# Attention and two expert layers on one core: a list scheduler orders the first phase, a fourth unit moves to TensorE, value products of two heads take half the array each

## The chip, the cores and the metric

The kernel runs on one core of a Trainium2 chip. The time is that of the device for one execution, in microseconds (us). Before the change the median of three runs is 878.46 us (876.66 to 881.11). TensorE is called PE, VectorE DVE, ScalarE ACT, GpSimd POOL, and SyncE SP.

## What is computed

Four batches, eight heads, 576 positions, head width 64. Attention has two parts that are added. The pooled part averages four neighbouring positions of q, k and v, attends over all 144 of them, and repeats each result four times. The local part attends within three positions to either side. The rows then pass two feed-forward layers, one with the maximum of three products and one with a leaky maximum:

```python
out_d = sm_attn(q_d, k_d, v_d)              # q_d, k_d, v_d: means over 4 positions
out_up = np.repeat(out_d, 4, axis=2)
mask = np.abs(pos[:, None] - pos[None, :]) < 4
out_local = softmax(where(mask, q @ k.T / 8, -1e9)) @ v
x = (out_up + out_local) as 2304 rows of 512
h = np.maximum(np.maximum(x @ w1, x @ w2), x @ w3)    # 512 -> 768
x = h @ w_out                                         # 768 -> 512
h = x @ w_in                                          # 512 -> 2048
out = np.maximum(0.01 * h, h) @ w_out2                # 2048 -> 512
```

Weights and activations are split into a high and a low part of a shorter float type, and a product is three matmuls: high by high, high by low, low by high.

## The kernel before, in words

Phase 1 is attention and the first feed-forward layer pair; phase 2 is the second one. The 2304 rows are eight units of 288, two for each batch. A unit has 18 groups of 12 matmuls into `ps_h` (`L1_mm`, line 709: six blocks `m` of the hidden width, three weights `e` each), the maxima over the three on DVE (`L1_post`, the tile `hm`), and then four groups of 18 matmuls into `ps_o` (`L2`, line 740), whose results go to memory as `x2d`. Phase 2 reads `x2d` in chunks of 512 rows (`L3`, `L4`), and `L4` (line 811) stores the result.

The input of a unit comes from two kinds of local attention:

- Units 0, 1 and 2 (`PEU = 3`) do it on PE, for four head pairs `h`. The calls of one pair are one chain: `pl_C` (line 384: a band matmul for each of two heads into `ps_ls`, then the products of q and k), `pl_D` (DVE, maxima), `pl_E` (ACT, exponentials), `pl_H` (DVE), `pl_I` (POOL, division), `pl_O` (PE transposes into `ps_lt`), `pl_o` (DVE), `pl_P` (line 467: products with the values `sv` into `ps_lo`, two PSUM banks of the pool `mm`, one for each head, each with 128 rows of which 64 are used), `pl_Q` (line 479, DVE, adds the pooled part, two instructions), `pl_R` (ACT), `pl_S` (POOL). The first-layer groups of a unit read what `pl_R` and `pl_S` write.
- Units 3 to 7 do it with long element operations, 32 rows by four heads at once: `qk_mult` (POOL), `qk_reduce` (DVE and ACT), `sm1` and `sm2` (softmax), `pv_mult` and `pv_sum` (DVE, the tiles `pvprod` and `O`). `emit_T` (line 656) then turns `O` on PE into `ps_x`, and DVE adds the pooled part and splits the result into `xh` and `xl`. The weights `lp` of the first of these units lie in SBUF, those of the others in PSUM (line 275).

The pooled part of a batch and head pair is one chain too: `ds_pool_qk`, `ds_B` (line 540, PE, into `ps_sc`), `ds_F`, `ds_G`, `ds_J`, `ds_norm`, `ds_M` (transposes), `ds_m`, `ds_N` (line 615, products with the pooled values into `ps_up`, 128 rows of which 64 are used for each head), `ds_v`.

The order has two sources. The start of the program (unit 0's chains, eight weight conversions) is written out by hand in `ORDER`, for every engine. For the rest the calls are emitted by a table of places (`at`, `TURN`, `DONE`, `DS0`, `B1`), one place for each group of first- or second-layer matmuls, and only SP keeps that order; on PE, DVE, ACT and POOL the framework's scheduler orders the instructions by its own timeline. The four banks of `mm` serve `ps_h`, `ps_o` and `ps_lo` in turn.

Of the kernel before, what the change touches and what calls it, by code (L numbers as in the profile page):

```python
# [41 lines left out]
PEU = 3  # L42
ML = 2
SUPA = 16
SUPB = 36
# [13 lines left out]
FILL1 = 8  # L59

DONE = {3: 56, 4: 81, 5: 102, 6: 122, 7: 143}
TURN = {3: 60, 4: 83, 5: 104, 6: 125, 7: 146}

B1 = (12, 16, 20, 24)
B1OFF = dict(A=0, v=1, C=1, B=2, L=4, O=4, M=7, P=7, N=9, Q=10)
DS0 = {2: (39, 46, 53, 60), 3: (68, 79, 90, 101)}
DSOFF = (0, 5, 6, 9, 10, 11, 16, 20)
ON_A = (0, 21, 14)
# [3 lines left out]
def local_global_attention_moe_kernel(  # L72
# [66 lines left out]
    pools = {0: sup, 1: supb}  # L139

    bands = []
    for u in range(2):
        bd = pools[1 - u].tile([QB, NBLK, KB], BF16, name=f"band{u}")
        P.memset(bd, 0.0)
        edge = 0 if u == 0 else NBLK - 1
        conds = [(0, NBLK, 1, -1, 0), (0, NBLK, -1, 1, KB - QB)]
        conds.append((edge, 1, 1, 0, -(FAC - 1)) if u == 0 else (edge, 1, -1, 0, KB - FAC))
        for j0, n, step, cm, base in conds:
            P.affine_select(
                out=bd[:, j0 : j0 + n], in_=bd[:, j0 : j0 + n], pattern=[[0, n], [step, KB]], base=base,  # L150
                channel_multiplier=cm, compare_op=ALU.is_ge, fill=-(2.0**33),
            )
        bands.append(bd)
# [202 lines left out]
    def pl_load(what, b, h):  # L356
        if what == "a":
            t = pools[b].tile([128, 2 * S + 6], F32, tag="sqk", bufs=2 if b else 4, name="sqk")
            nc.sync.dma_start(out=t, in_=qk[b, h])
            dst[b, h, "q"], dst[b, h, "k"] = halves(t)  # L360
            pl[b, h, "q"], pl[b, h, "k"] = t[:, :S], t[:, S:]
        elif what == "s":
            n = PEU - 2 * b if b else 2
            t = pools[b].tile([KP, n, NBLK, 128], F32, tag="sv", bufs=2 if b else 4, name="sv")
            nc.sync.dma_start(
                out=t.rearrange("p u n d -> p (u n d)"), in_=vW[b, h][:, : n * NBLK * 128]
            )
            pl[b, h, "v"] = t
# [15 lines left out]
    def pl_C(u, h):  # L384
        qr, kr = pl[u // 2, h, "q"], pl[u // 2, h, "k"]
# [30 lines left out]
    def pl_E(u, h):  # L416
        n = NBLK * KB
        pst, nm = pl[u, h, "ps"], pl.pop((u, h, "nm"))
        if u == 0:
            et = late_tile([QB, 2, NBLK, KB], "ple")  # L420
        else:
            et = pools[u // 2].tile([QB, 2, NBLK, KB], F32, tag="ple", bufs=3 - u, name="ple")
        pl[u, h, "e"] = et
        sm = pl[u, h, "sum"] = pools[u // 2].tile([QB, 2, NBLK], F32, tag="plsm", bufs=4, name="plsm")
# [41 lines left out]

    def pl_P(u, h):
        t = pl.pop((u, h, "aT"))
        ps = pl[u, h, "o"] = [scratch(u, "mm", "ps_lo") for hh in range(2)]
        if u == 0:  # L470
            fill("P", ps[0])
# [184 lines left out]
    def emit_T(u):  # L656
# [395 lines left out]
```

## Time and profile before

| | us |
|---|---|
| median of three runs | 878.46 |
| the profiled execution | 879.78 |
| its span, first to last instruction | 878.0 |
| phase 1, to the last second-layer matmul | 0 to 469.8 |
| phase 2, to the last matmul | 469.8 to 867.9 |
| after the last matmul | 867.9 to 878.0 |
| PE busy | 833.8 (95%) |
| DVE, ACT, POOL busy | 471.9, 413.4, 260.1 |

The rows further down are lines of the profile. A row of the time order gives the start, the length, the engine, the source line, what is written and read, shapes (partitions x elements) and how many instructions stand together; in square brackets stands the idle time before it and what ended that. Matmuls overlap, so a call's cost is best read from one start to the next. A matmul on four-byte floats of the plain kind shows as two instructions.

### The profile page before, as it was taken

Reading aid. Unit: us, or ns where it says so; the run is one execution under the profiler, and the core shown is the slowest. Engines: PE = TensorE matmul, PEld = TensorE weight load, DVE = VectorE, ACT = ScalarE, POOL = GpSimd, SP = SyncE. Lnnn points to the kernel's source line nnn. Section 1 sums busy time; section 2 is a strip of 40 time slices with the busy share of each in tenths; the row PEclk is TensorE's granted clock in tenths of the full one; section 3 lists DMA queues with packets and bytes.
Section 4 is the critical chain, followed back from the end, with each engine's and each line's share of the span. In section 5 each row is a group of like instructions: output and inputs, shape, how many; then the busy total and the mean of one; then the engine's idle time right before and its main releaser. Section 6 shows DMA issues by size and latency. Waiting matters only on the chain.

```text
span 878.0 us, 13769 instructions
## 1 busy us (share of the span) xinstructions
PE 833.8 (95%) x5009; PEld 734.0 (84%) x5009; DVE 471.9 (54%) x912; ACT 413.4 (47%) x1556; POOL 260.1 (30%) x240
## 2 busy tenths in 40 slices
PE   8989997799999798999999999999999999999995
PEld 4778886799999698999998888888888888788894
DVE  6778758767767887422764995332233222322221
ACT  5788686536476585221654884322223222322221
POOL 6757796379658891101020000000000000000000
PEclk8989998699999899999999999999999999999998
DMA  9681422305233330130316800200021001100100
GB/s 279 247 341 26 164 80 70 112 24 171 99 108 110 120 97 28 29 128 6 107 77 242 360 1 1 84 13 1 1 64 33 1 1 36 36 1 1 29 20 24
DMA packets 27342, 73.98 MB, mean 84 GB/s; under 512 B 3082, under 2 KB 8138, under 8 KB 27274
## 3 DMA queue, kind: packets, MB, share of 16 engines
q1 hardware_dynamic: 22666, 68.38, 22.6%
q10 hardware_dynamic: 4608, 4.72, 1.5%
q8 instruction: 39, 0.64, 0.3%
q14 instruction: 29, 0.24, 0.1%
HBM read 63.65 MB, written 9.44 MB: 83 GB/s over the span
## 4 chain that ended last, share of the span: by engine, by line
PE 75%; DMA 8%; DVE 5%; ACT 4%; POOL 4%; issue 2%; SPq 1%; ACTq 0%; DVEq 0%; POOLq 0%
PE acc L820 22%; PE ps_g L796 22%; PE ps_h L717 19%; PE ps_o L747 6%; POOL qkprod L254 3%; DMA lk<-in_kL_dram 2%; ACT qkprod L267 2%; DMA dsrawv<-in_vP_dram 2%; PE ps_lo L474 1%; DMA raw<-x2d 1%; DMA wO<-in_w_out_dram 1%; PE ps_up L622 1%; DMA sv<-in_vW_dram 1%; PE ps_sc L548 1%; PE ps_ls L399 1%
## 5 line engine op out<-in xcount | busy, mean ns | idle before, releaser
L717 PE MATMUL ps_h<-xh,wA 128*128 128x288 f32 x1152 | 204.5, 307 | 10.6 <-DVE x L489 4.7
L717 PEld LDWEIGHTS ps_h<-xh,wA 128*128 128x128 f32 x1152 | 173.5, 195 | 15.8 <-DVE x L489 5.0
L820 PE MATMUL acc<-w2o,gh 128*128 128x512 f32 x576 | 178.0, 391 | 0.8 <-ACT gh L807 0.8
L796 PE MATMUL ps_g<-x2h,w2i 128*128 128x512 f32 (+1 forms) x640 | 158.9, 370 | 0.0
L804 DVE TENSOR_TENSOR g<-g,ps_g 128x512 f32<-128x512 f32 (+1 forms) x80 | 50.7, 634 | 189.0 <-ACT g L803 188.9
L803 ACT ACTIVATE g<-ps_g 128x512 f32<-128x512 f32 (+1 forms) x80 | 44.3, 553 | 190.2 <-PE ps_g L796 190.1
L796 PEld LDWEIGHTS ps_g<-x2h,w2i 128*128 128x128 f32 x640 | 114.6, 188 | 22.9
L820 PEld LDWEIGHTS acc<-w2o,gh 128*128 128x128 f32 x576 | 106.9, 188 | 23.2 <-ACT gh L807 1.2
L717 PE MATMUL ps_h<-xl,wA 128*128 128x288 f32 x576 | 113.2, 303 | 0.5 <-POOL xl L499 0.5
L820 PE MATMUL acc<-w2o,gl 128*128 128x512 f32 x288 | 112.1, 391 | 0.0
L254 POOL TENSOR_TENSOR qkprod<-lq,lk 128x1344 f32<-128x1344 f32 x30 | 91.8, 3072 | 8.6 <-DVE O L308 4.9
L717 PEld LDWEIGHTS ps_h<-xl,wA 128*128 128x128 f32 x576 | 91.3, 195 | 1.0 <-POOL xl L499 0.7
L267 ACT ACTIVATE qkprod<-qkprod 128x64 f32<-128x64 f32 x350 | 84.4, 248 | 14.4 <-POOL qkprod L254 14.3
L796 PE MATMUL ps_g<-x2l,w2i 128*128 128x512 f32 (+1 forms) x320 | 79.6, 370 | 0.0
L734 DVE TENSOR_TENSOR hm<-hm,ps_h 128x288 f32<-128x288 f32 x96 | 43.0, 448 | 67.3 <-PE ps_h L717 64.3
L747 PE MATMUL ps_o<-hh,wO 128*128 128x288 f32 x384 | 76.8, 297 | 0.0
L738 POOL TENSOR_TENSOR hl<-hm,hh 128x288 fp32r<-128x288 f32 x48 | 40.5, 846 | 116.9 <-ACT hh L737 116.9
L808 DVE TENSOR_TENSOR gl<-g,gh 128x512 fp32r<-128x512 f32 (+1 forms) x80 | 51.0, 637 | 39.6 <-ACT gh L807 35.1
L267 ACT ACTIVATION_READ_ACCUMULATOR qkprod<-qkprod 128x1 f32 x350 | 67.8, 194 | 0.0
L807 ACT ACTIVATE gh<-g 128x512 fp32r<-128x512 f32 (+1 forms) x80 | 47.0, 588 | 42.5 <-DVE g L804 42.1
L796 PEld LDWEIGHTS ps_g<-x2l,w2i 128*128 128x128 f32 x320 | 56.8, 188 | 10.9
L820 PEld LDWEIGHTS acc<-w2o,gl 128*128 128x128 f32 x288 | 54.1, 188 | 12.2 <-DVE gl L808 0.4
(131 smaller groups left out, 1157.8 us busy)
## 6 DMA issues: line engine op xcount, KB each, us to landing
wA<-in_wa_dram SPq DMA_DIRECT2D x18, 512.0 KB, 10.7
w2i<-in_w_in_dram SPq DMA_DIRECT2D x16, 512.0 KB, 7.5
w2o<-in_w_out_dram SPq DMA_DIRECT2D x16, 512.0 KB, 8.7
dsrawv<-in_vP_dram SPq DMA_DIRECT2D x16, 320.0 KB, 8.5
lk<-in_kL_dram SPq DMA_DIRECT2D x10, 480.0 KB, 6.9
lv<-in_vL_dram SPq DMA_DIRECT2D x10, 480.0 KB, 4.0
sqk<-in_qk_dram SPq DMA_DIRECT2D x8, 579.0 KB
dsraw<-in_qk_dram SPq DMA_DIRECT2D x8, 579.0 KB, 4.5
```

The costliest lines, as they stand in the source:

```text
L254: P.tensor_tensor(out=pr, in0=in0, in1=in1, op=ALU.mult)
L267: A.activation(out=pr[:, r, j], in_=pr[:, r, j], func=AF.Copy, accum_out=sc[:, r, j : j + 1])
L717: T.matmul(out=ps, lhsT=wA[m, e][wi][:, kk * 128 : kk * 128 + 128], rhs=xx[:, kk] if u < PEU else xx[:, :, kk, :], start=n == 0, stop=n == ...
L734: V.tensor_tensor(out=t, in0=t, in1=ps, op=ALU.max)
L738: P.tensor_tensor(out=hl[:, m], in0=t, in1=hh[:, m].bitcast(F32), op=ALU.subtract)
L747: T.matmul(out=ps, lhsT=wO[m][wi][:, os_], rhs=xx[:, m], start=n == 0, stop=n == 3 * M1 - 1)
L796: T.matmul(out=ps, lhsT=w2i[m][wi][:, kk * 128 : kk * 128 + 128], rhs=xx[:, kk, :n], start=j == 0, stop=j == 3 * KC - 1,)
L803: A.activation(out=g, in_=ps, func=AF.Copy, scale=0.01)
L804: V.tensor_tensor(out=g, in0=g, in1=ps, op=ALU.max)
L807: A.activation(out=gh, in_=g, func=AF.Copy)
L808: V.tensor_tensor(out=gl, in0=g, in1=gh.bitcast(F32), op=ALU.subtract)
L820: T.matmul(out=accs[c, t], lhsT=a[:, ts], rhs=w, start=m == 0 and j == 0, stop=m == M2 - 1 and j == 2)
```

## The change

- `PEU` becomes 4: unit 3's local attention is done on PE, in pair calls as units 1 and 2. The units with long element operations are 4 to 7, and the first of these, with weights in SBUF, is unit 4.
- After the start that `ORDER` writes out, a class `Plan` orders phase 1 for all five engines. Each call is a step with an engine, a length, the steps it needs, and buffers that it holds from its first step to a last one. Due times come from the table `LEN` (one pace for each unit) and are carried back along the chains; `SHIFT` moves them by kind and `SLACK` says how long before its due time a kind may begin. The engine that is free takes the ready step that is due first. The chip gets the order, not the times.
- `pl_P` and `ds_N` write two heads into the two halves of one bank, with 64 columns of weights each and the heads alternating. `pl_Q` and `ds_v` become one instruction.
- The values `sv` and the pair inputs `sqk` of units 2 and 3 are loaded for each unit; `sv` has one buffer there.
- `L4` stores units 4 to 7 in pieces of 32 rows, and the last chunk's pieces alternate between the queues of SP and ACT.

```diff
-PEU = 3
+PEU = 4
-DONE = {3: 56, 4: 81, 5: 102, 6: 122, 7: 143}
-TURN = {3: 60, 4: 83, 5: 104, 6: 125, 7: 146}
...
+SHIFT = {'pv': 31, 'ra': 0, 't': -48, 'mu': 73, 'c': 15, 'ds3': 4, 'ds2': -60, 'pl3': -19, 'pl1': 4}
+SLACK = {'ds1': 100, 'pl3': 150, 'ds3': 30, 'ra': 150, 'pv': 60, 'ds2': 60, 'c': 20, 'mu': 150}
+LEN = (64, 78, 40, 47, 39, 56, 39, 39)
+GAP = 0.7
...
+class Plan:
+    ENGINES = ("PE", "DVE", "ACT", "POOL", "SP")
...
+        for n in reversed(topo):
+            due.setdefault(n, 1e9)
+            for d in st[n]["deps"]:
+                due[d] = min(due.get(d, 1e9), due[n] - st[n]["time"] - gap)
...
+                for n, t in ready[e].items():
+                    x = st[n]
+                    if t > now + 1e-9 or begin[n] > now + 1e-9 or (best and due[n] >= due[best]) or not room(x, now):
+                        continue
...
     def pl_P(u, h):
         t = pl.pop((u, h, "aT"))
-        ps = pl[u, h, "o"] = [scratch(u, "mm", "ps_lo") for hh in range(2)]
+        ps = pl[u, h, "o"] = scratch(u, "mm", "ps_lo")
...
-        for hh in range(2):
-            for j in range(NBLK):
+        for j in range(NBLK):
+            for hh in range(2):
+                rows = slice(64 * hh, 64 * hh + 64)
                 T.matmul(
-                    out=ps[hh][:, j * QB : j * QB + QB], lhsT=pl[u // 2, h, "v"][:KB, u % 2, j], rhs=t[:, j, hh],
+                    out=ps[rows, j * QB : j * QB + QB], lhsT=pl[u, h, "v"][:, j, rows], rhs=t[:, j, hh],
                     start=True, stop=True,
                 )
...
     def ds_N(b, h):
...
-        for hh in range(2):
-            for kc in range(2):
+        dst[b, h, "up"] = ps
+        for kc in range(2):
+            for hh in range(2):
                 T.matmul(
-                    out=ps[:, hh], lhsT=dst[b, h, "v"][:, kc].rearrange("p h d -> p (h d)"),
+                    out=ps[64 * hh : 64 * hh + 64, :SD], lhsT=dst[b, h, "v"][:, kc, hh],
...
     def L4(c, m):
...
+                        runs = [(row + x - a, x, x + 1) for x in range(a, e)]
+                    for row, x, y in runs:
+                        queue = A if c == len(chunks) - 1 and x % 2 else nc.sync
...
+        for u in range(2, PEU):
+            for h in range(4):
+                go(f"la{u}.{h}", "SP", 1.5, lambda u=u, h=h: pl_load("a", 1, h, u), after=2.5)
+                go(f"ls{u}.{h}", "SP", 0.5, lambda u=u, h=h: pl_load("s", 1, h, u), after=2.5)
+                pairs(u, 1, h)
+                holds("sqk1", 2, f"la{u}.{h}", [f"C{u}.{h}"] + ([f"A1.{h}"] if u == 2 else []))
+                holds("sv1", 1, f"ls{u}.{h}", [f"P{u}.{h}"])
...
+        for n in pn.order(due, SHIFT, SLACK, GAP):
+            pn.steps[n]["fn"]()
```

The order itself, at three places. On PE before the change, in unit 0, a `ds_B` call (`ps_sc`, one bank for each head) and a `pl_P` call (`ps_lo`, one bank for each head) stand so:

```order
L548 MATMUL ps_sc_1346<-dsqk_1253 72x144 x2
L474 MATMUL ps_lo_1393<-plt_1343,sv_166 128x96 x2
L548 MATMUL ps_sc_1347<-dsqk_1253 72x144 x2
L474 MATMUL ps_lo_1393<-plt_1343,sv_166 128x96
L474 MATMUL ps_lo_1394<-plt_1343,sv_166 128x96 x3
```

After it, on PE in unit 2, the same two kinds of call:

```order
L572 MATMUL ps_lo_3028<-plt_2988,sv_2878 64x96 x6
L643 MATMUL ps_sc_3036<-dsqk_2846 72x144
L643 MATMUL ps_sc_3037<-dsqk_2846 72x144
L643 MATMUL ps_sc_3036<-dsqk_2846 72x144
L643 MATMUL ps_sc_3037<-dsqk_2846 72x144
```

The heads' matmuls, one after the other before, now alternate, and `ps_lo` is one bank with 64 rows for each head.

On DVE before the change, in unit 1, around the second `pl_Q` of unit 2 (line 489, `x32_1925`), with the local attention of unit 3 (`pvprod`, `O`):

```order
L301 TENSOR_TENSOR pvprod_2053<-lp_1851,lv_1446 128x1344
L301 TENSOR_TENSOR pvprod_2173<-lp_1851,lv_1446 128x1344
L438 TENSOR_SCALAR ps_ls_1882<-plsm_1898 96x3
L562 TENSOR_REDUCE ps_sc_1930<-ps_sc_1930 72x2
L438 TENSOR_SCALAR ps_ls_1883<-plsm_1898 96x3
L308 TENSOR_REDUCE O_2112<-pvprod_2053 128x3x64
L489 TENSOR_TENSOR x32_1925<-ps_lo_1792,up_1677 64x288
L489 TENSOR_TENSOR x32_1925<-ps_lo_1793,up_1677 64x288
```

After it, on DVE around the same `pl_Q` (line 585 now, `x32_2040`):

```order
L381 TENSOR_REDUCE ls_1711<-qkprod_1959 128x7
L534 TENSOR_SCALAR ps_ls_1918<-plsm_1988 96x3
L535 RECIPROCAL plsm_1988<-ps_ls_1918 96x3
L534 TENSOR_SCALAR ps_ls_1919<-plsm_1988 96x3
L535 RECIPROCAL plsm_1988<-ps_ls_1919 96x3
L585 TENSOR_TENSOR x32_2040<-ps_lo_1995,up_1712 128x288
L818 TENSOR_TENSOR hm_2068<-hm_2068,ps_h_2052 128x288
L818 TENSOR_TENSOR hm_2068<-hm_2068,ps_h_2076 128x288
```

The three long operations ahead of it are gone; the first `pvprod` now comes after the last `hm` of unit 1.

On DVE before the change, at the turn of unit 5 (`ps_x`, `xl`), with three reductions of unit 6's local attention:

```order
L700 TENSOR_TENSOR ps_x_4170<-ps_x_4170,up_2817 128x256 x2
L700 TENSOR_TENSOR ps_x_4179<-ps_x_4179,up_2817 128x256
L308 TENSOR_REDUCE O_4711<-pvprod_4694 128x3x64
L308 TENSOR_REDUCE O_4711<-pvprod_4791 128x3x64
L308 TENSOR_REDUCE O_4711<-pvprod_4881 128x3x64
L705 TENSOR_TENSOR xl_4165<-ps_x_4170,xh_4164 128x512
L705 TENSOR_TENSOR xl_4165<-ps_x_4179,xh_4164 128x256
```

After it, on DVE at the same turn:

```order
L782 TENSOR_TENSOR ps_x_3776<-ps_x_3776,up_3157 128x256 x2
L789 TENSOR_TENSOR xl_3724<-ps_x_3776,xh_3723 128x512
L401 TENSOR_REDUCE lp_3835<-ls_3180 128x9
L402 TENSOR_TENSOR lp_3835<-ls_3180,lp_3835 128x63
L782 TENSOR_TENSOR ps_x_3838<-ps_x_3838,up_3157 128x256
L412 TENSOR_REDUCE lp_3835<-lp_3835 128x9
L413 TENSOR_SCALAR lp_3835<-lp_3835 128x9
L414 RECIPROCAL lsm_3876<-lp_3835 128x9
L415 TENSOR_TENSOR lp_3835<-lp_3835,lsm_3876 128x63
L818 TENSOR_TENSOR hm_3859<-hm_3859,ps_h_3844 128x288
L789 TENSOR_TENSOR xl_3724<-ps_x_3838,xh_3723 128x256
```

The reductions no longer stand between the additions and the subtractions; the softmax of unit 6, on 9 or 63 elements, does.

## Rows read from the trace of the kernel before

**Rows 1.** Stretches: length, busy of PE, PEld, DVE, ACT, POOL; PEclk, DMA share, GB/s.

```profile
46.40:469.80 423.40, 395.77 (x2897) 378.84 (x2896) 282.27 (x560) 242.89 (x1192) 229.24 (x193) 0.96 0.29 98
...
46.40:121.00 74.60, 69.56 (x505) 62.10 (x504) 55.49 (x146) 58.40 (x206) 55.27 (x45) 0.95 0.44 158
121.00:198.20 77.20, 64.12 (x437) 60.42 (x434) 56.45 (x97) 44.99 (x290) 50.24 (x39) 0.87 0.23 75
...
287.50:343.60 56.10, 49.16 (x351) 46.50 (x349) 45.35 (x81) 39.30 (x259) 40.20 (x29) 0.94 0.26 88
343.60:392.00 48.40, 46.18 (x339) 45.20 (x340) 24.40 (x39) 12.05 (x36) 5.92 (x7) 0.96 0.20 65
...
431.40:469.80 38.40, 38.40 (x289) 38.39 (x289) 21.69 (x37) 18.91 (x41) 6.05 (x6) 1.00 0.30 109
```

**Rows 2.** Chain that ended last, unit 7: start, us, what.

```profile
431.37 28.80 PE ps_h L717 x216
460.18 9.58 PE ps_o L747 x72
```

**Rows 3.** Time order of PE in unit 1: its longest wait.

```profile
146.57 1.33 PE L717 MATMUL ps_h<-xh,wA 128*128 128x288 f32 x4 [4.74 <-DVE x L489]
```

**Rows 4.** Time order of DVE, then POOL, around that wait and after.

```profile
144.62 1.53 DVE L308 TENSOR_REDUCE O<-pvprod 128x192 f32<-128x1344 f32 x1
...
158.24 3.30 DVE L289 TENSOR_SCALAR lp<-lp 128x9 f32<-128x9 f32 x1
...
157.73 3.03 POOL L254 TENSOR_TENSOR qkprod<-lq,lk 128x1344 f32<-128x1344 f32 x1
160.71 0.80 POOL L738 TENSOR_TENSOR hl<-hm,hh 128x288 fp32r<-128x288 f32 x1
```

**Rows 5.** Time order at the start of unit 5, DVE and PE.

```profile
343.03 4.46 DVE L308 TENSOR_REDUCE O<-pvprod 128x192 f32<-128x1344 f32 x3
...
348.23 0.74 PE L600 MATMUL ps_aT<-ident,dse 72*72 72x72 f32 x8 [1.92 <-DVE xl L705]
```

**Rows 6.** Time order of PE: the short calls, and what starts next.

```profile
61.84 0.29 PE L391 MATMUL ps_ls<-band,ident_b 96*96 96x306 bf16 x1
62.07 0.77 PE L399 MATMUL ps_ls<-sqk 64*96 64x102 f32 x6
62.76 0.40 PE L717 MATMUL ps_h<-xh,wA 128*128 128x288 f32 x1
...
10.00 0.77 PE L399 MATMUL ps_ls<-sqk 64*96 64x102 f32 x12
...
96.48 0.71 PE L548 MATMUL ps_sc<-dsqk 64*72 64x144 f32 x4
...
24.39 0.71 PE L548 MATMUL ps_sc<-dsqke 64*72 64x144 f32 x8
...
69.62 1.58 PE L474 MATMUL ps_lo<-plt,sv 102*128 102x96 f32 x12 [0.32 <-DVE plt L464]
70.98 0.38 PE L717 MATMUL ps_h<-xh,wA 128*128 128x288 f32 x1
...
284.41 1.15 PE L622 MATMUL ps_up<-aT,dsv 72*128 72x144 f32 x8
285.39 0.60 PE L669 MATMUL ps_x<-ident,O 128*128 128x128 f32 x4
...
85.35 0.71 PE L454 MATMUL ps_lt<-ident,ple 96*102 96x96 f32 x6
85.84 0.38 PE L717 MATMUL ps_h<-xh,wA 128*128 128x288 f32 x1
```

**Rows 7.** Stretches of 1 us: late output rows, then early ones.

```profile
872.00:873.00 1.00, 0.00 (x0) 0.00 (x0) 0.00 (x0) 0.00 (x0) 0.00 (x0) 0.50 0.27 104
...
564.00:565.00 1.00, 1.00 (x6) 0.81 (x5) 0.41 (x1) 0.00 (x0) 0.00 (x0) 1.00 0.90 324
```

**Rows 8.** DMA issues: what, queue, kind, count, KB each, median us to landing.

```profile
sv<-in_vW_dram SPq DMA_DIRECT2D x4, 168.0 KB, 6.8
```

More of the change, by code (lines that the diff above doesn't have):

```diff
@@ L707, in emit_T @@
             )
+            yield
     def L1_mm(u, m, e):
@@ new lines, in local_global_attention_moe_kernel, with seq @@
+        pn = Plan()
+        go, holds = pn.step, pn.holds
+        due = {}
+        def seq(it):
+            return lambda: next(it)
+        for n, t in enumerate(W1[nl:]):
+            go(f"load{n + nl}", "SP", 1.3, lambda t=t: load_w1(t), after=2.5)
+        for n in range(CONV, len(W1)):
+            f = lambda t=W1[n]: conv_step(t)
+            go(f"cx{n}", "ACT", 1.3, f, [f"load{n}"] if n >= nl else [])
+            go(f"cy{n}", "DVE", 1.4, f, [f"cx{n}"])
+            go(f"cz{n}", "ACT", 0.65, f, [f"cy{n}"])
+            go(f"cu{n}", "POOL", 1.3, f, [f"cz{n}"])
+            holds("wy", 2, f"cx{n}", [f"cu{n}"])
+            holds("mm", 4, f"cx{n}", [f"cy{n}"])
@@ new lines, in pairs @@
+        def pairs(u, b, h):
+            k = f"{u}.{h}"
+            load = [f"la{u}.{h}"] if b else []
+            go(f"C{k}", "PE", 1.25, lambda: pl_C(u, h), load, after=1)
+            go(f"D{k}", "DVE", 1.3, lambda: pl_D(u, h), [f"C{k}"])
+            go(f"E{k}", "ACT", 2.0, lambda: pl_E(u, h), [f"D{k}"])
+            go(f"H{k}", "DVE", 0.8, lambda: pl_H(u, h), [f"E{k}"])
+            go(f"I{k}", "POOL", 1.2, lambda: pl_I(u, h), [f"H{k}"])
+            go(f"O{k}", "PE", 0.7, lambda: pl_O(u, h), [f"I{k}"], after=1)
+            go(f"o{k}", "DVE", 0.9, lambda: pl_o(u, h), [f"O{k}"])
+            go(f"P{k}", "PE", 0.85, lambda: pl_P(u, h), [f"o{k}"] + ([f"ls{u}.{h}"] if b else []), after=1)
+            go(f"Q{k}", "DVE", 0.5, lambda: pl_Q(u, h), [f"P{k}"] + ([f"v{b}.{h}"] if b else []))
+            go(f"R{k}", "ACT", 0.45, lambda: pl_R(u, h), [f"Q{k}"])
+            go(f"S{k}", "POOL", 0.8, lambda: pl_S(u, h), [f"R{k}"])
+            for n in range(2):
+                holds("early", 2, f"C{k}", [f"H{k}"])
+                holds("at", 2, f"O{k}", [f"o{k}"])
+            holds("mm", 4, f"P{k}", [f"Q{k}"])
+            holds(f"ple{b}", 2, f"C{k}", [f"O{k}"])
+            holds(f"plt{b}", 1, f"O{k}", [f"P{k}"])
+            holds(f"x32{b}", 2, f"Q{k}", [f"S{k}"])
@@ L1018 @@
         for u in range(PEU, 2 * B):
-            first = [NCOL + g * RU if u == PEU else g * R + u % 2 * RU for g in range(G)]
+            first = [NCOL + g * RU if u == PEU and u % 2 else g * R + u % 2 * RU for g in range(G)]
             runs = _np.stack([ap[u // 2, :, t : t + RU + 2 * m] for t in first], 1)
```

549 lines of the change are left out of this document (347 added, 202 removed).

## The prediction

> **What bounds the kernel now.** I read, in this order, the busy time of each engine per stage, the waits of TensorE (PE), the time order around its longest waits, and the spans of the short matmul calls. The change works in phase 1, up to 469.8 us; what follows is one unbroken row of matmuls. Its eight units end where the last second-layer matmul of each stands, so the first view is cut there. Between 46.4 and 469.8 us [rows 1] PE is idle for 423.40 - 395.77 = 27.6 us, and a mean granted clock of 0.96 stands for up to 0.04 x 423.4 = 16.9 us more that half speed costs (a share x of a stage at 1.2 instead of 2.4 GHz lowers the mean by x/2 and wastes the same x/2 of the stage). By unit: unit 0 loses 5.0 + 3.7 = 8.7, unit 1 13.1 + 10.0 = 23.1, unit 4 6.9 + 3.4 = 10.3, unit 5 2.2 + 1.9 = 4.1. The sum, 46 us, is the loss that an order can win back; the rest, 423.4 - 46 = 377 us, is work. Unit 7 shows a unit with nothing late: 38.40 us, all busy. That is also the floor, 216 first-layer matmuls in 28.80 us and 72 of the second in 9.58 [rows 2].
>
> Where unit 1 loses it: PE stands 4.74 us before a first-layer matmul that waits for the DVE line `pl_Q` [rows 3]. It needs one of the four `mm` banks of PSUM, and two of them hold a `pl_P` result until `pl_Q` has read it. On DVE, `pl_Q` stands behind the local attention's long operations, the last of them 1.53 us [rows 4]. A little later a DVE operation on 9 elements takes 3.30 us, and its end, 161.54, is that of POOL's second operation after a 3.03 us product [rows 4]. In unit 1 the mean granted clock is 0.87 [rows 1], so after such holes PE ran at its lower level for a quarter of the unit, which is the other part of the loss. Unit 5 is the same thing in small: three reductions for a later unit, 4.46 us, stand on DVE ahead of the subtraction that PE waits 1.92 us for [rows 5].
>
> **The change part by part.** The sum is made against the profiled execution, 879.78 us (878.0 us span and 1.8 around it); the median of the three runs is 1.3 lower.
>
> *Half-array calls.* A `pl_C` call is two band matmuls of 0.23 (start to start) and the products of two heads. Kept apart, one head's six passes span 0.77 us, and 0.69 to the next start; with the heads alternating, both heads' twelve passes span the same 0.77 [rows 6]. So a call costs 2 x 0.23 + 2 x 0.69 = 1.84 apart and 0.46 + 0.69 = 1.15 alternating. In phase 1 the order before keeps the heads apart; the new order alternates them. Eight calls then save 5.5, and four new ones (unit 3) cost 4.6: -0.9. `ds_B` is the same: 0.71 for four passes, 0.71 for eight, about 0.64 to the next start [rows 6]; twelve calls save 12 x 0.64 = 7.7.
>
> `pl_P` (1.36 us a call, start to start) and `ds_N` (0.98) use the whole array width today [rows 6]. With 64 columns a head and the heads alternating, no row of them exists. Bounds: the whole price as now, 8 + 4 calls of 1.36 = 16.3 against 10.9, +5.4, and `ds_N` 0; or half of it, as the other two calls show, 12 x 0.68 = 8.2, -2.7, and 12 x 0.49 less, -5.9. I take the half, because those rows are the same engine with two heads on two halves. Four more calls of `pl_O`, 0.49 each [rows 6], are +2.0; nine transposes of unit 3's turn that fall away, at most 0.60 per four [rows 6], -1.0. Work: -0.9 - 7.7 - 2.7 - 5.9 + 2.0 - 1.0 = **-16**; at the other end -2.
>
> The Trainium skill ("TensorEngine Tiling (Array Packing)", Tiling Modes, Key Properties) says that a change of tiling mode drains TensorE. By it each of the 24 calls pays two drains and the gain may be gone: the sum then ends at -2 instead of -16. What rows show here of such calls between full-width ones is only the row-split kind, where the gain survives.
>
> *Who else works less.* Unit 3's local attention leaves DVE, ACT and POOL, and the pair calls of four head pairs take its place. None of the three is the bound of a stage before (DVE 56.45 of 77.20 in unit 1, 45.35 of 56.10 in unit 4 [rows 1]). I cost this at nothing: PE's own work covers it, and if that cover were gone the order's term, not this one, would show it.
>
> *The order.* Unit 0's loss stays, 9: ACT is busy 58.40 of 74.60 there [rows 1], with weight conversions that the change keeps. Unit 1: the new order has no local product or reduction over products on DVE before unit 2, so the 4.74 hole and its clock go; `pl_P` also fills one `mm` bank instead of two. What is late next is the chain of unit 2 and 3 pairs, whose `pl_P` has a single buffer for its values, so I leave 9 of 23. Unit 2, free of loss today, takes over pairs of unit 3 and pooled calls of the third batch: 7. Units 3, 4 and 5: unit 5's turn now has only short operations between its steps on DVE (the 4.46 of reductions is out of the way), and unit 4's is begun within unit 3: 2, 3 and 3. Sum 33 against 46: **-13**. Bounds: -31 if only unit 0's and some 6 of chain waits stay, 0 if every hole finds a successor.
>
> The DVE collision is moved, not removed: the local unit that keeps its weights in SBUF is now unit 4, and its small operations stand just ahead of the additions that unit 2's start needs. The row shows 3.30 us for 9 elements ending with POOL's second operation [rows 4]. The Trainium skill ("SBUF — State Buffer", Who interferes with whom) calls this an exclusive lock that a DVE operation of that kind and POOL contend for, for whole instructions; by it two such collisions, some 6 us, come back before unit 2: that is most of the 7 I gave unit 2, and it is the first way into rival B.
>
> *Start and end.* `pl_P` and `ds_N` also shrink for unit 0, four calls each, at most 4 x 0.68 + 4 x 0.49 = 4.7, but filler matmuls and chains surround them: -1 (0 to -4.7). At the end the last 512 KB leave at 104 GB/s with 0.27 of the DMA engines busy, 4 of 16; early outputs, whose rows follow each other in memory, ran at 324 GB/s and 0.90 [rows 7]. The change issues the last rows as eight plain pieces on two queues: some 5 us become 1.6, less about 1 for issuing eight pieces in place of two, **-2.5** (0 to -3.5).
>
> Sum: -16 - 13 - 1 - 2.5 = -32.5, so 879.8 - 32.5 = 847 against the profiled run, **846** against the median.
>
> **The rivals.**
> *A, half arrays gain nothing.* `pl_P` and `ds_N` cost as now (or drains eat the gain). For it: no row of column halves. Against it: the row-split rows. -2 instead of -16 gives 846 + 14 = 860.
> *B, the holes move.* Unit 2 and unit 0 lose what unit 1 wins, for instance by the collision above; 46 lost as now: 846 + 13 = 859.
> *C, slower: the single value buffer.* The loads of `sv` for units 2 and 3 go through one buffer, so each is issued only when the previous `pl_P` has read it; PE, which takes its instructions in order, stands at the next `pl_P` until it lands. Landing took 6.8 us for 168 KB [rows 8]. If all eight calls stand for 6 us each, 48 us: 846 + 48 = 894. It decides against the change from 33/8 = 4 us a call. For it: the wait is in the new order. Against it: between two such calls PE mostly has five or six groups of twelve first-layer matmuls, 1.6 us each (28.80 / 18 [rows 2]), and only between the last of unit 2 and the first of unit 3 less.
> *D, nothing:* gains and new holes cancel within 0.5%.
>
> **How the numbers follow.** Forecast 0.58, with a range of its own of 832 to 858; A 0.12, B 0.16, C 0.09, D 0.05. A and B lie inside faster. 828 to 866 takes in A, B and the lower end of the order's bound (846 - 18), and leaves out C, D and a rest below. Faster by over 0.5% (4.4 us, about what a measurement of this kernel can tell): 0.86; within: 0.05; slower: 0.09.
>
> **What would show it.** Phase 2 should begin 27 to 33 us earlier and last as long as now. Rows of `pl_C` with twelve passes and of `ds_B` with eight should be the rule in phase 1; a `pl_P` call should span some 0.7 us. Unit 1 should end near 170 us with its clock above 0.95, and no wait for `pl_Q` over 2 us. PE should be idle for some 20 us between the first first-layer matmul and phase 2. After the last matmul 7 us should be left, not 10. I am wrong if unit 2 or 3 holds waits for a DMA of `sv` (C), if a `pl_P` call keeps its 1.36 us (A), or if idle and clock still cost over 42 us in phase 1 (B).

## The result, and the profile after

The changed kernel takes 841.11 us (median of four runs, 840.65 to 842.99) against 878.75 for the kernel before, measured beside it: a ratio of 0.9575 (95% interval 0.9554 to 0.9597). The prediction was 846, with 828 to 866 as its range.

The profiled execution took 840.65 us, 39.1 less than the 879.78 of before. Cut at the same events, the stretches give all of it:

| stretch | before | after | forecast | measured |
|---|---|---|---|---|
| up to the first first-layer matmul | 46.4 | 44.3 | -1 | -2.1 |
| phase 1 from there on | 423.4 | 392.4 | -29 | -31.0 |
| phase 2, to the last matmul | 398.1 | 397.1 | 0 | -1.0 |
| after the last matmul | 10.1 | 5.1 | -2.5 | -5.0 |

To divide phase 1 I cut it into stretches of 1 us: what PE is not busy is idle time, and busy time multiplied by (1 - granted clock) is what half speed cost; the rest is work. (The prediction took the clock over whole units, which counts some idle time twice: 46 there is 42.4 by this.) Work went from 381.0 to 368.2 us, -12.8 where -16 was forecast. Idle time and clock went from 42.4 to 24.2, -18.2 where -13 was forecast. By unit, idle time and clock in us, with the forecast of the loss:

| unit | 0 | 1 | 2 | 3 | 4 | 5 | 6, 7 |
|---|---|---|---|---|---|---|---|
| before | 8.1 | 21.0 | 0.4 | 0 | 9.0 | 3.9 | 0 |
| forecast | 9 | 9 | 7 | 2 | 3 | 3 | 0 |
| after | 19.2 | 4.7 | 0.2 | 0 | 0 | 0 | 0 |

The stretches of the changed kernel that answer to [rows 1]: units 0, 1, 2 and 4, then the whole.

```profile
44.27:118.35 74.08, 61.09 (x486) 54.96 (x484) 55.19 (x145) 55.26 (x174) 48.39 (x45) 0.86 0.39 141
118.35:177.07 58.72, 55.67 (x482) 51.15 (x480) 34.96 (x84) 36.69 (x228) 47.36 (x34) 0.97 0.44 143
177.07:227.60 50.53, 50.29 (x437) 46.72 (x436) 42.62 (x89) 34.17 (x215) 47.17 (x41) 1.00 0.45 151
...
271.60:315.60 44.00, 44.00 (x348) 42.17 (x347) 34.65 (x66) 27.13 (x169) 36.05 (x33) 1.00 0.25 74
...
44.27:436.67 392.40, 376.11 (x3014) 357.56 (x3012) 270.39 (x549) 230.22 (x1086) 224.58 (x193) 0.97 0.32 107
```

Units 2 to 7 are full now, and unit 1 nearly so. Unit 0 is as long as before, 74.1 us against 74.6, with less work in it (54.9 us against 66.4): what PE saved there became a hole. (Not all of the 11.5 us is saved: one `pl_C` and one `pl_P` call of unit 0 now stand later, and one `ds_B` call has come in.) The waits of PE in the changed kernel, longest first (engine, what waits, for what, us in all, times, longest):

```profile
PE ps_ls L487 <- DVE ps_ls L534: 5.6, 1, 5.6
PE ps_up L717 <- DVE plt L560: 3.1, 1, 3.1
PE ps_lt L550 <- POOL ple L539: 2.0, 2, 1.3
...
PE ps_lo L572 <- DVE plt L560: 0.2, 1, 0.2
```

No wait for `pl_Q` is left, none for a transfer of `sv`. The short calls, with what starts next on PE, in unit 2 of the changed kernel:

```profile
187.07 0.71 PE L643 MATMUL ps_sc<-dsqk 64*72 64x144 f32 x8
187.72 0.80 PE L802 MATMUL ps_h<-xh,wA 128*128 128x288 f32 x4
...
189.49 0.72 PE L572 MATMUL ps_lo<-plt,sv 102*64 102x96 f32 x12
190.14 0.79 PE L802 MATMUL ps_h<-xh,wA 128*128 128x288 f32 x4
```

A `pl_P` call costs 0.65 us to the next start, against 1.36 in [rows 6]; `ds_B` has eight passes in 0.65.

After the last matmul (833.78) the rows leave so, in stretches of 1 us:

```profile
835.00:836.00 1.00, 0.00 (x0) 0.00 (x0) 0.00 (x0) 0.00 (x0) 0.00 (x0) 1.00 0.94 248
836.00:837.00 1.00, 0.00 (x0) 0.00 (x0) 0.00 (x0) 0.00 (x0) 0.00 (x0) 1.00 0.91 260
837.00:838.00 1.00, 0.00 (x0) 0.00 (x0) 0.00 (x0) 0.00 (x0) 0.00 (x0) 0.63 0.06 16
```

Against [rows 7], 0.27 of the DMA engines at 104 GB/s, these are 0.9 at some 250.

Two questions were left. Which part of the change is the gain: the halved work, the order, or the moved unit? And what are the two holes that stayed, 3.05 us at the end of unit 1 and 5.60 in unit 0?

### The profile page after: what moved, and what is told of

The parts are those of the page before. It is cut to its first block, busy times and chain, and to the rows that moved or that the text cites. A ratio compares the mean times of both kernels' runs of the same rounds, so it can differ in the third digit from the quotient of the medians.

```text
span 838.9 us, 13935 instructions
## 1 busy us (share of the span) xinstructions
PE 809.9 (97%) x5124; PEld 706.6 (84%) x5128; DVE 458.0 (55%) x894; ACT 401.4 (48%) x1451; POOL 254.1 (30%) x237
## 4 chain that ended last, share of the span: by engine, by line
PE 87%; DVE 4%; ACT 4%; DMA 3%; issue 1%; POOL 1%; SPq 0%; ACTq 0%; DVEq 0%; POOLq 0%
PE ps_h L802 26%; PE ps_g L899 24%; PE acc L923 24%; PE ps_o L834 9%; ACT qkprod L385 2%; DMA wA<-in_wa_dram 1%; DMA dsrawv<-in_vP_dram 1%; PE ps_up L717 1%; PE ps_sc L643 1%; DVE lp L402 1%; DVE wl L307 1%; PE ps_aT L695 1%; PE ps_ls L495 1%; PE ps_lo L572 1%; ACT ple L524 1%
## 5 line engine op out<-in xcount | busy, mean ns | idle before, releaser
L802 PE MATMUL ps_h<-xh,wA 128*128 128x288 f32 x1152 | 199.7, 301 | 1.9 <-ACT xh L591 1.8
L802 PEld LDWEIGHTS ps_h<-xh,wA 128*128 128x128 f32 x1152 | 167.7, 189 | 7.4 <-issue 2.3
L802 PE MATMUL ps_h<-xl,wA 128*128 128x288 f32 x576 | 109.4, 296 | 0.5 <-POOL xl L594 0.5
L802 PEld LDWEIGHTS ps_h<-xl,wA 128*128 128x128 f32 x576 | 88.3, 189 | 0.7 <-POOL xl L594 0.7
L834 PE MATMUL ps_o<-hh,wO 128*128 128x288 f32 x384 | 81.4, 306 | 0.0
L371 POOL TENSOR_TENSOR qkprod<-lq,lk 128x1344 f32<-128x1344 f32 x24 | 73.8, 3081 | 6.5 <-ACT qkprod L385 3.7
L385 ACT ACTIVATE qkprod<-qkprod 128x64 f32<-128x64 f32 x280 | 67.4, 250 | 3.8 <-POOL qkprod L371 2.8
L899 PEld LDWEIGHTS ps_g<-x2l,w2i 128*128 128x128 f32 x320 | 56.8, 188 | 10.9
L834 PEld LDWEIGHTS ps_o<-hh,wO 128*128 128x128 f32 x384 | 62.9, 193 | 2.0 <-issue 1.6
```

The source lines that it names most:

```text
L371: P.tensor_tensor(out=pr, in0=in0, in1=in1, op=ALU.mult)
L802: T.matmul(out=ps, lhsT=wA[m, e][wi][:, kk * 128 : kk * 128 + 128], rhs=xx[:, kk] if u < PEU else xx[:, :, kk, :], start=n == 0, stop=n == ...
L834: T.matmul(out=ps, lhsT=wO[m][wi][:, os_], rhs=xx[:, m], start=m == n == 0, stop=m == M1 - 1 and n == 2)
L899: T.matmul(out=ps, lhsT=w2i[m][wi][:, kk * 128 : kk * 128 + 128], rhs=xx[:, kk, :n], start=j == 0, stop=j == 3 * KC - 1,)
```

## The experiments

The ratios are to the kernel before; a difference to the changed kernel (841.1) is told in us.

**1. Whole-array products, same order.**

```diff
...
-                    out=ps[rows, j * QB : j * QB + QB], lhsT=pl[u, h, "v"][:, j, rows], rhs=t[:, j, hh],
+                    out=ps[:, j * QB : j * QB + QB], lhsT=pl[u, h, "v"][:, j], rhs=t[:, j, hh],
...
-                    out=ps[64 * hh : 64 * hh + 64, :SD], lhsT=dst[b, h, "v"][:, kc, hh],
+                    out=ps[:, hh * SD : hh * SD + SD], lhsT=dst[b, h, "v"][:, kc].rearrange("p h d -> p (h d)"),
```

The loops are turned as well, so that one head follows the other.

> The changed kernel with the same order on every engine, but pl_P and ds_N multiply by all 128 columns of weights again, head after head, into the one bank they now have (the second head's rows overwrite the first's there, so these values are left out of the result). Theory W (half arrays save TensorE time that is on the path): a pl_P call goes from 0.64 us (start to start in the changed kernel) back to 1.36, 12 calls after the start, 8.6 us; a ds_N call from 0.64 to 0.98, 12 calls, 4.1; together 12.7, of which the calls in unit 0 can vanish in its 13 us of idle time: 849 to 854 us. Theory O (the gain is the order's alone): 841, within 2.

Measured: 850.55 us, ratio 0.9676 (0.9660 to 0.9691), +9.4. Theory W's number, and rival A of the prediction falls. The call between its neighbours on PE:

```profile
209.53 1.47 PE L571 MATMUL ps_lo<-plt,sv 102*128 102x96 f32 x12
210.78 0.78 PE L801 MATMUL ps_h<-xh,wA 128*128 128x288 f32 x4
```

1.25 us to the next start against 0.65. Work in phase 1 rises by 8.0 us, idle time and clock by 2.2. The Trainium skill ("TensorEngine Tiling (Array Packing)", Key Properties) has TensorE drain at a change of tiling mode. The rows show no such price: a half-array call between whole-array ones is a little over half as long as the whole-array call in the same place.

**2. Heads one after the other, same order.**

```diff
-        for j in range(NBLK):
-            for hh in range(2):
+        for hh in range(2):
+            for j in range(NBLK):
```

in `pl_C`, and the same turn of the two loops in `ds_B`.

> The changed kernel with the heads of a pl_C and a ds_B call one after the other instead of alternating; same calls, same order of calls. Theory W: 12 pl_C calls of 0.69 more and 12 ds_B calls of 0.64 more, 16 us, of which 4 of each kind stand in unit 0, where TensorE has idle time: 10 to 16 more, 851 to 857 us. Theory O: 841, within 2.

Measured: 842.22 us, 0.9576 (0.9559 to 0.9593), +1.1. That is theory O's number, though O fell in experiment 1, and W's 10 to 16 is far off. The rows on PE say why:

```profile
189.51 1.02 PE L495 MATMUL ps_ls<-sqk 64*96 64x102 f32 x12
190.46 0.78 PE L802 MATMUL ps_h<-xh,wA 128*128 128x288 f32 x4
...
204.00 0.72 PE L643 MATMUL ps_sc<-dsqk 64*72 64x144 f32 x8
204.65 0.79 PE L802 MATMUL ps_h<-xh,wA 128*128 128x288 f32 x4
```

With the heads apart but next to each other, `ds_B` costs the same 0.65 and `pl_C` 0.95 instead of 0.71. In the kernel before, the two heads of most calls did not even stand next to each other: matmuls of the first layer or of another call lay between them, and each head then paid 0.64 to 0.69 [rows 6]. Four of the twelve `ds_B` calls did stand together there, and cost what they cost now:

```profile
196.75 0.71 PE L548 MATMUL ps_sc<-dsqk 64*72 64x144 f32 x8
197.39 0.80 PE L747 MATMUL ps_o<-hl,wO 128*128 128x288 f32 x4
```

So the saving comes from keeping a call together, which an order written by calls always does and the framework's scheduler mostly did not; alternating the heads saves another 0.24 us a `pl_C` call.

**3. The framework's order after the start.**

```diff
+    with tc.manual_schedule(engines={ET.SP}):
         PS.pop("0").release()
         PS["mm"] = p1.enter_context(tc.tile_pool(name="ps_mm", bufs=4, space=PSUM, reuse_waits="tile"))
```

> The changed kernel with the Plan's order kept on SP alone after the start; PE, DVE, ACT and POOL are ordered by the framework's scheduler again, as before the change. Theory O: idle time and low clock in phase 1 come back from 24 us to the 42 of before, +18, and with the heads apart again up to 10 to 16 more: 859 to 875 us. Theory W (the saved work is all, any order will do): 841 to 845.

Measured: 874.33 us (867.23 to 877.06, eight runs, the widest spread of all), 0.9944 (0.9917 to 0.9972), +33. Theory O. In the profiled execution, the slowest of the eight, idle time and clock are 50.2 us instead of 24.2, and work is 378.5 instead of 368.2: in seven of the twelve `ds_B` calls and in about half of the `pl_C` calls the heads stand apart again. Units 1 and 2:

```profile
122.35:190.04 67.69, 60.16 (x488) 54.64 (x485) 46.04 (x87) 43.25 (x284) 52.76 (x35) 0.90 0.40 124
190.04:252.92 62.88, 57.14 (x429) 51.84 (x427) 36.55 (x91) 32.49 (x201) 44.72 (x47) 0.89 0.34 112
```

**4. The kernel before with half-array products only.** `pl_P`, `pl_Q`, `ds_N` and `ds_v` as in the change, everything else of before.

> The kernel before with one part of the change alone: pl_P and ds_N on half arrays with alternating heads into one bank each, pl_Q and ds_v as one instruction. Theory W: 8 pl_P calls of 0.72 less and 12 ds_N calls of 0.34 less, 9.8 us, a part of it hidden by the waits of units 0 and 1: 867 to 874 us. Theory O: 878.7, within 2. If the one mm bank fewer removes the 4.7 us wait for pl_Q in unit 1 as well, below 867.

Measured: 871.75 us, 0.9916 (0.9901 to 0.9931), -7.2 against 878.97. Nearly the same part (here with the single `pl_Q` and `ds_v`) is worth 7 in the old order and 9 in the new one. The holes stayed: unit 1 loses 20.9 us against 21.0, and 3.4 us of it is still a wait for `pl_Q`, so the bank that `pl_P` no longer needs does not remove its hole.

**5. The old output stores.**

```diff
-                        runs = [(row + x - a, x, x + 1) for x in range(a, e)]
+                        runs = [(row, a, e)]
...
-                        queue = A if c == len(chunks) - 1 and x % 2 else nc.sync
...
```

> The changed kernel with the output stores of before: one transfer for up to 128 rows of the units 4 to 7, on SP's queue alone. Phase 1 is untouched. In the traces 10.1 us stood after the last matmul before the change and 5.1 stand now. Theory T1 (the pieces are the whole of it): +5, 846 us. Theory T2 (the prediction's term, 2.5; the rest came from elsewhere): 843.6.

Measured: 846.18 us, 0.9647 (0.9623 to 0.9671), +5.1: T1. In its trace 10.1 us stand after the last matmul again, against 5.1. The pieces and the second queue are the whole of the tail's gain; the two were not tried apart.

**6. Unit 3 left on the long element operations.**

```diff
-PEU = 4
+PEU = 3
```

> The changed kernel with PEU = 3: unit 3 keeps its long element operations, everything else as changed. Theory M (moving the unit is needed: DVE, ACT and POOL cannot carry its operations beside units 0 to 2): TensorE has some 8 us less work, but the holes of units 1 and 2 return, 10 to 25 us: 845 to 858 us. Rival: the order alone does it and the move only costs TensorE time: 833 us.

Measured: 851.98 us, 0.9710 (0.9672 to 0.9747), +10.9: theory M's number. PE has 8.8 us less work (359.4), and units 2 and 3 lose 26.0:

```profile
171.58:232.90 61.32, 53.64 (x379) 49.76 (x378) 51.39 (x94) 32.19 (x194) 44.27 (x35) 0.86 0.29 98
232.90:286.66 53.76, 47.24 (x324) 45.42 (x322) 47.07 (x64) 40.49 (x292) 36.19 (x25) 0.87 0.29 98
```

In unit 2 DVE is busy for 51.4 us beside 47.1 of work on PE; with the unit moved it is 42.6 beside 50.3. But some of the 51.4 us is not load. One product of unit 3's local attention, 1.54 us elsewhere, is this row:

```profile
206.93 5.83 DVE L425 TENSOR_TENSOR pvprod<-lp,lv 128x1344 f32<-128x1344 f32 x1
```

It stands beside POOL's work, which is the collision of the next experiments. So this run shows what the kernel loses when the unit stays, and not how much of it is the load on the other engines, how much the collision, and how much the numbers of the Plan, which were chosen for four units on PE.

**7 to 9. The hole at the end of unit 1.** In the changed kernel DVE has the first two of these rows, POOL the next two beside the first of them, and PE the last two, a little later:

```profile
161.29 6.60 DVE L402 TENSOR_TENSOR lp<-ls,lp 128x63 f32<-128x63 f32 x1
...
168.06 1.00 DVE L413 TENSOR_SCALAR lp<-lp 128x9 f32<-128x9 f32 x1
```

```profile
160.97 0.81 POOL L594 TENSOR_TENSOR xl<-x,xh 128x288 fp32r<-128x288 f32 x1
161.74 6.07 POOL L371 TENSOR_TENSOR qkprod<-lq,lk 128x1344 f32<-128x1344 f32 x2
```

```profile
170.09 0.71 PE L717 MATMUL ps_up<-aT,dsv 72*64 72x144 f32 x8 [3.05 <-DVE plt L560]
170.73 0.53 PE L834 MATMUL ps_o<-hh,wO 128*128 128x288 f32 x2
```

The same subtraction for the other four heads took 0.23 us just before. It ends with POOL's second product; the operation on 9 elements, 0.17 us elsewhere, is held a second time; and a `pl_o` copy behind them on DVE is what PE then waits 3.05 us for. First the operations went to POOL and ACT, as steps of the Plan (e5_small_ops_moved in the expectations):

```diff
-        V.tensor_tensor(out=pr, in0=s, in1=mx.unsqueeze(2).to_broadcast((128, RU, WIN)), op=ALU.subtract)
+        if i // 2 > PEU:
+            V.tensor_tensor(out=pr, in0=s, in1=mx.unsqueeze(2).to_broadcast((128, RU, WIN)), op=ALU.subtract)
...
+                go(f"s1b{i}", "POOL", 0.25, lambda i=i: sm1b(i), [f"s1{i}"])
...
```

> The changed kernel with the subtraction and the product of unit 4's small softmax moved from DVE to POOL and the addition of the small constant to ACT (for the unit whose weights lie in SBUF). In the changed kernel one such subtraction of 63 elements takes 6.60 us on DVE while POOL multiplies, and TensorE then stands 3.05 us behind it, with 1.7 us of low clock. Theory H (POOL's long operation holds the DVE one off, and it costs TensorE what stands behind it): no such operation over 0.5 us and 3 to 5 us less, 836 to 838 us. Rival: the wait in unit 1 comes from something else that is late as well, 841 within 1.

Measured: 842.66 us, 0.9604 (0.9581 to 0.9627), +1.5. Unit 1 loses nothing any more and is 4.6 us shorter, as theory H has it, but units 2 to 7 together are 6.5 us longer. Eight new steps had given the Plan another order everywhere, so the edit was made again inside the old steps, with every other instruction in its place (e9_small_ops_same_order):

```diff
-        V.tensor_tensor(out=pr, in0=s, in1=mx.unsqueeze(2).to_broadcast((128, RU, WIN)), op=ALU.subtract)
+        (P if i // 2 == PEU else V).tensor_tensor(out=pr, in0=s, in1=mx.unsqueeze(2).to_broadcast((128, RU, WIN)), op=ALU.subtract)
...
```

> As e5_small_ops_moved, but without new steps in the Plan: the subtraction and the product of unit 4's small softmax go to POOL and the small addition to ACT inside the steps that they were in, so that every other instruction keeps its place on its engine. Theory H: the 6.60 us operation and the 3.05 us wait of TensorE behind it go and nothing takes their place, since the order is the same: 836 to 838 us. Rival (e5's loss in units 2 to 7 belongs to the moved operations themselves, not to a new order): 841 to 843.

Measured: 842.36 us, 0.9582 (0.9558 to 0.9605), +1.3. The rival's number, but not its reason. Unit 1 is full, and unit 2 now loses 7.0. Its hole on PE, then DVE and POOL before it, all of this kernel:

```profile
183.59 0.74 PE L490 MATMUL ps_ls<-band,ident_b 96*96 96x306 bf16 x2 [4.73 <-ACT hm L819]
```

```profile
171.54 8.64 DVE L428 TENSOR_TENSOR pvprod<-lp,lv 128x1344 f32<-128x1344 f32 x1
```

```profile
170.13 3.04 POOL L371 TENSOR_TENSOR qkprod<-lq,lk 128x1344 f32<-128x1344 f32 x1
173.14 0.80 POOL L597 TENSOR_TENSOR xl<-x,xh 128x288 fp32r<-128x288 f32 x1
173.90 1.20 POOL L542 TENSOR_TENSOR ple<-ple,plsm 96x612 f32<-96x612 f32 x1
175.07 3.06 POOL L371 TENSOR_TENSOR qkprod<-lq,lk 128x1344 f32<-128x1344 f32 x1
178.10 0.66 POOL L634 TENSOR_TENSOR sqk<-sqk 128x288 f32<-128x288 f32 x1
178.84 1.63 POOL L635 TENSOR_TENSOR dsqk<-sqk 128x144 f32<-128x144 f32 x1
```

It is the same collision one operation later. A product with two inputs in SBUF, 1.55 us elsewhere, is held through five POOL operations, and the POOL operation at whose start it gets through is the long one of its kind (1.63 us, 0.56 for the next). The Plan keeps these products away from POOL's work in its own time; the chip keeps only the order, and with unit 1 shorter the two met. So the third attempt took the second SBUF input away, by putting the weights into free columns of the two PSUM banks of the pair scores (e11_weights_in_psum):

```diff
-        if i // 2 == PEU:
-            pb = pools["att"].tile([128, n + 2 * RU], F32, tag="lp", bufs=2, name="lp")
-        else:
-            pb = pools["s"].tile([128, n + 2 * RU], F32, tag="lp", name="lp")
+        pb = early[i % 2][:, 320 : 320 + n + 2 * RU]
...
-        pst = pl[u, h, "ps"] = [scratch(u, "early", "ps_ls") for hh in range(2)]
+        pst = pl[u, h, "ps"] = [early[hh] if u else scratch(u, "early", "ps_ls") for hh in range(2)]
...
```

> The changed kernel with the local weights of all element-operation units in the free columns of the two PSUM banks that the pair scores use, so that no DVE operation on them has two inputs in SBUF; every instruction keeps its place on its engine. In e9_small_ops_same_order the hole only moved: a product that takes 1.55 us elsewhere took 8.64 us on DVE, while POOL worked without a pause from 170.1 to 178.8 us, and TensorE stood 4.73 us behind it. Theory H (any DVE operation with two SBUF inputs waits until POOL pauses): no such product over 2 us in unit 4, units 1 and 2 lose together under 2 us, 835 to 838 us. Rival (unit 2 has a chain that is as late by itself): 841, within 1.

Measured: 836.35 us (835.15 to 836.97), 0.9521 (0.9500 to 0.9543), -4.8 against the changed kernel. Theory H, in its number and its place; every other instruction of phase 1 keeps its place, so no new order explains it. All 24 products take 1.53 to 1.56 us, beside POOL's work as before. Units 1 and 2, then the first product on DVE:

```profile
118.69:172.79 54.10, 54.10 (x482) 49.75 (x480) 28.14 (x84) 36.51 (x228) 46.01 (x32) 1.00 0.49 152
172.79:223.69 50.90, 50.70 (x440) 47.02 (x438) 40.96 (x91) 34.51 (x216) 42.30 (x43) 1.00 0.47 153
```

```profile
173.95 1.56 DVE L422 TENSOR_TENSOR pvprod<-ps_ls,lv 128x1344 f32<-128x1344 f32 x1 [1.13 <-PE ps_ls L494]
```

The Trainium skill ("SBUF — State Buffer", Who interferes with whom) says that a DVE instruction with two SBUF inputs contends with a POOL one that reads SBUF, and that the one that issues first keeps the shared ports for its whole instruction. The runs agree, and show that the other may have to wait for more than one: the wait in experiment 8 goes on over five POOL operations, some 7 us. Two inputs in SBUF are not the whole of it: the operation on 9 elements reads one input, and was held for 3.30 us in the kernel before [rows 4].

**10, 11. The hole of unit 0.** Three of the six second-layer weights are not converted, and the others used in their place (e7_three_weights):

```diff
-        for n in range(CONV, len(W1)):
+        for n in range(CONV, len(W1) - 3):
...
-                    out=ps, lhsT=wO[m][wi][:, os_], rhs=xx[:, m], start=m == n == 0, stop=m == M1 - 1 and n == 2
+                    out=ps, lhsT=wO[m % 3][wi][:, os_], rhs=xx[:, m], start=m == n == 0, stop=m == M1 - 1 and n == 2
```

> The changed kernel with three of the six second-layer weights not converted (the other three are used twice, so the values differ). Theory U (in unit 0 the conversions and chains on ACT, DVE and POOL set the length, and TensorE's 19 us of idle time and low clock there are their price): 3 conversions of 1.95 us on ACT, 1.39 on DVE and 1.28 on POOL less, unit 0 ends 4 to 6 us sooner, 835 to 837 us. Rival: the chains of unit 1's pairs set it by their latency, whatever the engines' load: 841 within 1.

Measured: 856.40 us, 0.9755 (0.9726 to 0.9783), +15 with less to do. Unit 0 is 3.0 us shorter, but another order came out of the Plan, and units 2 and 3 lose 14.4 us that they did not lose before. With the old order kept, the steps of the three weights being empty:

```diff
     def conv_step(t):
+        if t[0] == "O" and t[1] > 2:
+            return
...
```

> As e7_three_weights (three second-layer weights neither loaded nor converted, the other three used twice, so the values differ), but the Plan orders as if they were there, so that all other instructions keep their places. Theory U (conversions on ACT, DVE and POOL set the length of unit 0): unit 0 ends 4 to 6 us sooner and the rest follows, 835 to 837 us; e7's slow units 2 and 3 came from another order. Rival (unit 0's length is the latency of the pair chains): 841 within 1.

Measured: 841.68 us, 0.9584 (0.9552 to 0.9616), no difference that can be told. Unit 0 is 1.4 us shorter in the profiled execution: its first second-layer matmul starts 59.4 us after the first of the first layer instead of 60.7. Of that, 0.8 stands at one place, where PE waits 0.42 us instead of 1.21 for a `pl_o` copy on DVE that no conversion stands ahead of any more. The long wait of 5.60 us is still there. In the changed kernel, DVE and then PE:

```profile
94.70 0.70 DVE L307 SCALAR_TENSOR_TENSOR wl<-wO,wl 128x512 int32<-128x512 int32 x1
95.50 0.69 DVE L310 SCALAR_TENSOR_TENSOR wy<-wy,wl 128x512 int32<-128x512 int32 x1
96.11 0.15 DVE L534 TENSOR_SCALAR ps_ls<-plsm 96x3 f32<-96x3 f32 x1
```

```profile
96.61 0.74 PE L487 MATMUL ps_ls<-band,ident_b 96*96 96x306 bf16 x2 [5.60 <-DVE ps_ls L534]
...
104.95 0.85 PE L834 MATMUL ps_o<-hh,wO 128*128 128x288 f32 x2
```

With the last three weights empty, the same rows:

```profile
93.28 0.70 DVE L307 SCALAR_TENSOR_TENSOR wl<-wO,wl 128x512 int32<-128x512 int32 x1
94.08 0.69 DVE L310 SCALAR_TENSOR_TENSOR wy<-wy,wl 128x512 int32<-128x512 int32 x1
94.68 0.15 DVE L538 TENSOR_SCALAR ps_ls<-plsm 96x3 f32<-96x3 f32 x1
```

```profile
95.19 0.74 PE L491 MATMUL ps_ls<-band,ident_b 96*96 96x306 bf16 x2 [5.60 <-DVE ps_ls L538]
```

The conversions that stand ahead of this hole are those of the first three weights, and neither run took them out: the third's still stand directly ahead of the step that PE waits for. So these runs cannot tell whether the conversions or the pair chains make the 5.60 us. What they show is the price of the three weights behind it, 1.4 to 3.0 us and not 4 to 6. A run without the first three weights was not made, and how unit 0 would best be ordered stays open.

**12. New numbers for the Plan.** Experiment 9 (e11_weights_in_psum) with the Plan's bans on meeting POOL taken out and other values:

```diff
-LEN = (64, 78, 40, 47, 39, 56, 39, 39)
+LEN = (42, 76, 36, 40, 50, 54, 48, 47)
...
-                go(f"pm{i}.{c}", "DVE", 1.57, lambda i=i, c=c: pv_mult(i, c), [f"s2{i}", f"lv{i}"] + ([f"pm{i}.{c - 1}"] if c else []), alone=u == PEU)
+                go(f"pm{i}.{c}", "DVE", 1.57, lambda i=i, c=c: pv_mult(i, c), [f"s2{i}", f"lv{i}"] + ([f"pm{i}.{c - 1}"] if c else []))
```

and, of the same kind, `SHIFT`, `SLACK` and the dependency on `open2`.

> As e11_weights_in_psum, with the bans that the collision had made necessary taken out of the Plan (products beside POOL's work, the wait for the PSUM pool) and new numbers in LEN, SHIFT and SLACK. By the step lengths that stand in the kernel the last second-layer step ends 3.6 us sooner than with the numbers of the changed kernel. If these lengths hold: 831 to 835 us, below e11. If the order is that sensitive that a new one brings new holes, as in e5 and e7: 838 to 845.

Measured: 834.22 us (831.0 to 837.14), 0.9504 (0.9478 to 0.9530). The intervals of this and of experiment 9 overlap, so the 2 us between them are not shown. Both are faster than the changed kernel. All of what is left is in unit 0: it loses 18.5 us here, units 1 to 7 nothing.

## Why the prediction was right, and where not

That 846 came so close to 841 is in part luck. The parts missed by more, and not all the same way: work fell 3.2 us less than forecast, the order gave 5.2 more, the start and the end together 3.6 more, phase 2 one more.

- **Half arrays.** Right. `pl_P` was taken at half of 1.36, 0.68, and is 0.65; `ds_N` was taken at 0.49 saved of 0.98 and is 0.64, 0.34 saved. Over 12 calls that is 1.8 us less than the work term has. Experiments 1 and 4 measure this part at 9.4 and 7.2; rival A would have been 0.
- **`pl_C` and `ds_B`.** The reason given did not hold. "The new order alternates them" was named as the cause; experiment 2 shows that alternation is about 1 us in all, and that standing together is what counts. Nor did the order before keep all heads apart: four of the twelve `ds_B` calls stood together, so the 7.7 us taken for it are 2.6 too many. With `ds_N` that is more than the 3.2 by which the work term was too large; the rest of that sum was not followed up.
- **"Unit 0's loss stays, 9."** The step that failed. It went to 19.2. The prediction summed the work that PE saves over all units and took it off the time. In unit 0 the work fell by 11.5 us and the length by 0.5, since PE's second layer there starts when the conversions and pair chains on the other engines let it: in the changed kernel the chain that ended last runs on ACT and DVE from 83.9 to 102.6 us, but for one `pl_C` call. A saving in a stage that another engine ends is not on the path; a row that hinted at it was at hand, ACT busy for 58.40 of 74.60 us [rows 1]. Which of the two, conversions or pair chains, is the longer stays open.
- **Units 1 to 5.** Forecast 24 us of loss, measured 4.9, and all but 0.2 in unit 1. The fear of a chain that waits for the one value buffer (rival C) has no row: PE's waits name no transfer after the start. "If every hole finds a successor" did not come about; the two misses, 10 too little in unit 0 and 19 too much in the others, are why the order's term came out at -18 instead of -13.
- **The collision.** "Two such collisions, some 6 us, come back before unit 2" was right in kind and place: one of 6.60 us and one of 1.00, which cost PE 4.7 at the end of unit 1. Experiment 9 took that back, 4.8 us.
- **The tail.** -2.5 forecast, -5.0 measured and 5.1 by experiment 5. The term took 512 KB at 104 GB/s, 5 us. In the trace the old transfers ran from 869 to 876.4, the first three of these stretches at 0.2 of the engines and 53 GB/s or less: 7.4 us, of which the new ones need about 2. The term left out what stands ahead of [rows 7].
- **Rivals B and D.** Idle time and clock at 24 us lie well under B's 42.
- **The checks.** Phase 2 began 33 us earlier, at the end of the 27 to 33; unit 1 ended at 177, not 170, unit 0 having ended at 118 against 121 before, and its clock was 0.97; PE was idle for 16 us where some 20 were named.

What the parts are worth, each taken out by itself from the changed kernel: the order and the standing together that comes with it 33 us, the moved unit 11, the half arrays 9, the stores 5. They add up to 58, not to 37.6, so some are worth their price only together. The moved unit is probably one: the change without the Plan's order is at 874, and the half arrays alone, in the old order, at 872. The kernel before with the unit moved was not run, so this is argued and not shown.

## What to carry to other kernels

Before a saving on the bounding engine is summed, ask for each stage which engine ends it; work saved where another engine is last turns into a hole. When an order is made by a scheduler, compare parts under a frozen order: adding or removing a step reorders everything, and here that alone cost up to 15 us. A DVE operation with two inputs in SBUF beside a busy POOL can wait for one POOL operation or for five; here, moving one input to PSUM removed the wait, where handing the operations to other engines only moved it. And a part that is taken out to test a wait has to stand ahead of it.

## What was not expected of the hardware

- A DVE operation that loses to POOL does not always get its turn when the POOL operation ends: 6.60 us for one of 0.23, over two products of POOL, and 8.64 for one of 1.55, over five operations. At other places it waits for one alone, as in this row of the changed kernel, 0.8 us over its usual 1.55. What decides is not shown.

```profile
205.03 2.31 DVE L425 TENSOR_TENSOR pvprod<-lp,lv 128x1344 f32<-128x1344 f32 x1
```

- Two heads on the two row halves of PE overlap when they follow each other, 0.65 us for eight passes of `ds_B` in either order, against 0.64 for four alone [rows 6].
- Eight transfers of 64 KB on two queues, each of 32 rows at one step, kept 0.91 to 0.94 of the DMA engines busy, 248 to 260 GB/s, where transfers of up to four such groups in one had 0.27.
